# Order of the loads on GpSimd's queue in an attention and mixture kernel: q and k ahead of v, weight halves behind

## The chip, the cores and the metric

The kernel runs on one core of a Trainium2 chip. The metric is the device time of one execution in microseconds. The engines are called as in the profile: PE (matrix products), DVE (vector), ACT (activations and copies), POOL (GpSimd) and SP. All loads are issued by POOL, and their descriptors go to one queue; SP issues the stores of the result.

## The reference

An attention with an extra term in the denominator, for 8 batches of 12 heads with 448 tokens of 64 values, and behind it a soft mixture of 8 experts with 4 slots each. Cut to what matters:

```
scores = q @ k.T / sqrt(64);  m = max(scores);  e = exp(scores - m)
attn = e / (sum(e) + exp(-m) + 1e-9);  x = attn @ v          # x: 3584 x 768
logits = x @ phi                                             # 3584 x 32
d = softmax over the tokens;  slot_in = d.T @ x               # 32 x 768
slot_out[e] = relu(slot_in[e] @ w1[e]) @ w2[e]                # w1: 768x1024, w2: 1024x768
out = softmax over the slots(logits) @ slot_out
```

## The kernel before, in words

The work is cut into 48 pairs of heads, and three pairs make a group g (16 groups, two for each batch). One slot s of the main loop (L556) does the work of one pair, in two halves y; the order of the instructions on every engine is the order in which the code writes them, since the schedule is made by hand. The main parts are these:

- T(n) (L193) transposes q and k of pair n on PE: 14 transposes of q, then 14 of k, for 7 parts of the tokens and the two heads. In slot s from 2 on, y = 1 calls T(s + 6), so the transposes run six pairs ahead of the pair's exponentials.
- A(n, i) (L216) computes scores on PE (L225, L235) and takes their maxima on DVE (L229, L238). W1(g) (L241) writes the negated maxima of a group on POOL (L245), W2 and W3 turn them (PE L265, L266, ACT L271).
- Bk(n, i) (L281) computes the transposed scores less the maxima on PE (L300, L303) and the exponentials on ACT (L306); AV (L319) multiplies them with v on PE (L331).
- N1 and N2 (L337, L346) divide by the sums: a copy on ACT (L343), two small operations on DVE (L352, L353), three on POOL (L359, L367, L368). PX (L382) turns the result. P(b) (L404) does the logits of a batch in steps that are spread over later slots; its subtractions are on POOL (c_sub L437, d_sub L449), and the exponential of what they write is on ACT (L454).
- V(g) (L310) copies v of a group on POOL (L312 to L315) into a padded layout. It is called in each slot with s % 3 == 0.

The loads stand between these on POOL's stream. load(g, "q") and load(g, "k") (L141) fetch a whole group, cast to 16 bits, into one of two buffers, chosen by g % 2; T(n) reads it. load(g, "v") (L145, L146) fetches v into one buffer, from which V copies. The 16 weight matrices come as halves: the first eleven into a tile W of their own, a first half with load_half(i, 0) in the slots s = 1, 4, 7, 10, 13, 16, 22, 25, 28, 31, 34 and the second half one slot later (L108); the other five go into the space of R when attention has left it (from s = 38 on).

At the end of each slot, POOL gets its loads in this order (L607 to L626): in slots with s % 3 == 0, V, then v for the group after, then q and k of group s / 3 + 3; in slots with s % 3 == 1 (after W1) a first weight half; in slots with s % 3 == 2 a second half. q and k of group 3 are loaded in slot 1. POOL works through its stream in order, so an issue that waits holds up everything behind it.

After the main loop come the last products of P (L468), the experts (hidden L646, turn L657, slots L663), and the combination with the result's stores (L715 to L737).

Of the kernel before, what the change touches and what calls it, by code (L numbers as in the profile page):

```python
# [31 lines left out]
def kernel(  # L32
# [22 lines left out]
    NG = NPAIR // NP  # L55
# [45 lines left out]
    def w_view(i, t):  # L101
        kind, e = halves[i]
        w_sb[(kind, e)] = t.rearrange("p (j f) -> p j f", f=F if kind == "w1" else DD)

    def load_part(i, z0, z1):
        kind, e = halves[i]
        src = (moe_w1 if kind == "w1" else moe_w2)[e].rearrange("(j p) f -> p j f", p=128)
        gdma(out=w_sb[(kind, e)][:, z0:z1, :], in_=src[:, z0:z1, :])  # L108

    def load_half(i, z, t=None):  # L110

        if t is not None:
            w_view(i, t)
        n = (KC if halves[i][0] == "w1" else FK) // 2
        load_part(i, z * n, (z + 1) * n)
# [6 lines left out]
    with ExitStack() as at:  # L122
# [10 lines left out]
        def load(g, nm, l0=0, l1=NP):  # L133


            b, h0 = g // 2, (g % 2) * HG
            src = {"q": q, "k": k, "v": v}[nm][b, h0:h0 + HG]
            if nm != "v":
                t = part(f"nq{g % 2}", "qk".index(nm) * NP * S, NP * S).rearrange("p (l x) -> p l x", l=NP)
                x = src.rearrange("(l h) (j t) d -> (h j) l (t d)", h=2, t=7)  # L140
                gdma(out=t[:, l0:l1, :], in_=x[:, l0:l1, :])  # L141
            else:
                t = part("nv", 0, NATV).rearrange("p (h t d) -> p h t d", h=HG, t=4)
                x = src.rearrange("h (p t) d -> p h t d", t=7)
                gdma(out=t[0:64], in_=x[:, :, 0:4, :])  # L145
                gdma(out=t[64:128], in_=x[:, :, 3:7, :])  # L146
            nat[nm, g] = t
# [45 lines left out]
        def T(n):  # L193
            g, pl = divmod(n, NP)
            ps = psA.tile([128, 2, S], BF16, tag="a", name="ps_t")
            for a in range(2):
                src = nat["qk"[a], g]
                for tok in range(7):
                    for hl in range(2):

                        c = kcol(hl, tok) if a else (2 * tok if tok < 4 else 2 * tok - 7) * 64
                        r = slice(64 * hl, 64 * hl + 64)
                        nc.tensor.transpose(ps[r, a, c:c + 64], src[r, pl, tok * D:(tok + 1) * D], ident[r, r])  # L203
            t = qk_t[n % NQK]
            if n < 6 or pl == 0:
                nc.scalar.copy(t, ps)  # L206
            else:
                nc.vector.tensor_copy(t, ps)
            qkT[n] = t
# [31 lines left out]
        def W1(g):  # L241
            w, m = wm[g % 2], mx[g]
            l0, l1 = mpl(g)
            nm = psm.tile([128, 21], BF16, tag="ngm", name="ngm")
            neg = lambda o, s: nc.gpsimd.tensor_scalar(o, s, -1.0, None, op0=ALU.mult)  # L245
            cols = lambda t: t[:, 0:3 * HG].rearrange("p (i c) -> p i c", i=3)[:, :, 2 * l0:2 * l1]
            o = w[:, 0:3, :].rearrange("p i (d c) -> p i d c", d=2)[:, :, :, 2 * l0:2 * l1]
            neg(o, cols(m).unsqueeze(2).to_broadcast([128, 3, 2, 2 * (l1 - l0)]))
            for hl in range(2):
                r = slice(64 - 64 * hl, 128 - 64 * hl)  # L250
                o = w[r, 3, :].rearrange("p (d c) -> p d c", d=2)[:, :, 2 * l0 + hl:2 * l1:2]
                neg(o, m[r, 3 * HG + l0:3 * HG + l1].unsqueeze(1).to_broadcast([64, 2, l1 - l0]))
            if l1 - l0 == NP:
                neg(nm, m)
            else:
                nc.gpsimd.memset(nm, 0.0)
                neg(cols(nm), cols(m))
                neg(nm[:, 3 * HG + l0:3 * HG + l1], m[:, 3 * HG + l0:3 * HG + l1])
            ngm[g] = nm
# [21 lines left out]
        def Bk(n, i, c=0):  # L281

            g, pl = divmod(n, NP)
            t = qkT[n]
            rs = [slice(0, 64), slice(64, 128)]
            if i < 3:
                pss = [pb_("ps_b") for _ in range(2)]
                outs = [p[:, 0:S] for p in pss]
                cols = slice(i * 128, (i + 1) * 128)
                e = e2_t[st["e2"] % NE]  # L290
                st["e2"] += 1
                es = [e[:, hl, :] for hl in range(2)]
            else:
                pss = [pb_("ps_b")]
                outs = [pss[0][r, 0:S] for r in rs]
                cols = slice(384, 448)
                es = [e1_t]
            m = cols.stop - cols.start
            for hl in range(2):
                nc.tensor.matmul(outs[hl], t[rs[hl], 1, cols], t[rs[hl], 0, :], start=True, stop=False)  # L300
            As(c)
            for hl in range(2):
                nc.tensor.matmul(outs[hl], sel[rs[hl], 2 * pl + hl:2 * pl + hl + 1].to_broadcast([64, m]), mT[mg(n)][rs[hl], :],  # L303
                                 start=False, stop=True)
            for p, e in zip(pss, es):
                nc.scalar.activation(e, p[:, 0:S], AF.Exp, scale=scale)  # L306
            for hl in range(2):
                eT[n, i, hl] = es[hl % len(es)]
# [221 lines left out]
        def As(c):  # L530
            for _ in range(min(c, len(runs))):
                A(*runs.pop(0))
# [19 lines left out]
        half_at = {s: i for i, s in enumerate((1, 4, 7, 10, 13, 16, 22, 25, 28, 31, 34))}  # L552
# [3 lines left out]
        for s in range(NPAIR + 1):  # L556
            for y in range(2):
                hs = 2 * s + y
                early = int(hs < 5)
                As(1)  # L560
                if s < NPAIR:
                    Bk(s, 2 * y)
                    As(early)
                    side = int(y == 1 and len(runs) > 0 and runs[0][1] == 3)
                    Bk(s, 2 * y + 1, side)
                    As(1 - side)
                else:
                    As(1)
                if hs == 1:
                    W1(1)  # L570
                if hs < 5:
                    T(hs + 3)
                if y == 0:
                    if 0 <= s - 1:
                        for i in (2, 3):
                            AV(s - 1, i, range(3))
                else:
                    if 2 <= s < NPAIR - 6:
                        T(s + 6)
                    g = (s + 1) // 3  # L580
                    if (s + 1) % 3 == 0 and g < NG:
                        W2(g + 1)
                        W3(g + 1)
                    if s < NPAIR:
                        for i in (0, 1):
                            AV(s, i, range(3))
                if 2 * s + y in post:
                    post[2 * s + y]()
                if y and 0 <= s - 2 < NPAIR - 2:
                    PX(s - 2)  # L590
                if y == 0:
                    if 0 <= s - 1:
                        for i in range(4):
                            AV(s - 1, i, [3])
                        N1(s - 1)
                        if not on_pool(s - 1):
                            N2(s - 1)
                else:
                    if 0 <= s - 1 and on_pool(s - 1):
                        N2(s - 1)  # L600
                As(early)
                if hs == 1:
                    W2(1)
                    W3(1)
                if hs == 4:
                    W1(2)
            g = (s + 9) // 3  # L607
            if s % 3 == 0 and g - 2 < NG:
                V(g - 2)
                if s and g - 1 < NG:  # L610
                    load(g - 1, "v")
            if s == 1 or (s and s % 3 == 0):
                if g < NG:
                    load(g, "q")
                    load(g, "k")
            if s % 3 == 1:
                if 1 < (s + 2) // 3 < NG:
                    W1((s + 2) // 3 + 1)
                if s == 1:
                    load(2, "v")  # L620
            if s in half_at:
                load_half(half_at[s], 0, w_tile(half_at[s]))
            if s - 1 in half_at:
                load_half(half_at[s - 1], 1)
            for i, z0, z1 in part_at.get(s, ()):
                load_part(i, z0, z1)  # L626
        load_part(14, 1, 8)
# [140 lines left out]
```

## Time and profile before

| | |
|---|---|
| median of 3 runs | 326.14 us (326.11 to 327.19) |
| the profiled execution | 328.46 us |
| its span, first to last instruction | 326.7 us |
| busy share: PE, DVE, ACT, POOL | 86%, 79%, 77%, 61% |
| mean granted clock of PE | 0.96 |
| share of 16 DMA engines taken by the loads' queue | 85.1% |
| loads of q or k of a whole group: each, median from issue to landing | 336 KB, 7.1 us (q), 8.1 us (k) |
| half of a weight matrix | 768 KB, 9.2 us |

How to read it: busy times are those of one profiled execution. A timeline row has start and length in us, engine, line and operation, and in brackets how long the engine stood idle before it and what ended that. A row of the chain has start, length and what was working. A row of waits has who waited for what, us in total, how many times, and the longest. The size of a load is what it writes (16 bits a value); it reads twice that. A windows row has the stretch, its length, the busy time of PE, PE's weight loads, DVE, ACT and POOL with counts of instructions, the granted clock, the share of the DMA engines and GB/s.

### The profile page before, as it was taken

How to read it: one execution, taken by the hardware profiler on the slowest of the kernel's cores; microseconds unless marked ns; L12 is line 12 of the kernel's file. 1: busy time of each engine (PE TensorE's matmuls, PEld its weight loads, DVE VectorE, ACT ScalarE, POOL GpSimd, SP SyncE). 2: the span in 40 equal slices, each digit the busy share in tenths (PEclk: the TensorE clock that was granted, in tenths of full speed). 3: DMA queues.
4: the chain of work that ended last, by engine and by line, in shares of the span. 5: the costliest groups of instructions: out<-in, count | busy, mean ns of one | idle time of the engine just before them, and what ended most of it. 6: DMA issues, size and time to landing. Idle time of an engine off the chain costs nothing.

```text
span 326.7 us, 12121 instructions
## 1 busy us (share of the span) xinstructions
PE 281.9 (86%) x5054; PEld 162.9 (50%) x5054; DVE 257.8 (79%) x601; ACT 251.1 (77%) x547; POOL 198.1 (61%) x399
## 2 busy tenths in 40 slices
PE   3898899899999999899989999999999987987800
PEld 1444456556556565556555655556564544452100
DVE  5779999798999899889988998999999365337910
ACT  2457699989999899889988999899989986317800
POOL 8640769777778868585978597859666734100000
PEclk9999999999999999999999999999999999999555
DMA  7990699999999999759999999999934899983997
GB/s 93 131 132 3 91 208 149 203 171 170 158 181 169 183 176 158 102 64 175 137 181 169 171 153 177 170 184 142 144 50 70 136 153 176 210 159 148 442 421 337
DMA packets 42438, 54.30 MB, mean 166 GB/s; under 512 B 2576, under 2 KB 35344, under 8 KB 42000
## 3 DMA queue, kind: packets, MB, share of 16 engines
q0 software_dynamic: 41376, 42.52, 85.1%
q1 hardware_dynamic: 1008, 11.01, 8.0%
q8 instruction: 39, 0.64, 0.7%
q14 instruction: 15, 0.12, 0.1%
HBM read 85.03 MB, written 11.01 MB: 294 GB/s over the span
## 4 chain that ended last, share of the span: by engine, by line
PE 32%; DVE 24%; ACT 11%; POOL 11%; DMA 11%; issue 6%; POOLq 0%; ACTq 0%; DVEq 0%
DVE mx L229 14%; DMA R<-in_k_dram 11%; PE ps_av L331 6%; ACT R L306 5%; PE ps_a L225 5%; PE ps_b L300 4%; PE ps_t L203 4%; PE ps_b L303 3%; DVE mx L238 2%; ACT W L732 2%; PE ps_o L726 2%; ACT R L206 2%; PE ps_h L653 2%; PE ps_so L667 2%; PE ps_s L469 2%
## 5 line engine op out<-in xcount | busy, mean ns | idle before, releaser
L229 DVE TENSOR_REDUCE mx<-ps_a 128x1 f32<-128x448 f32 x288 | 160.4, 613 | 15.7 <-PE ps_a L225 15.2
L306 ACT ACTIVATE R<-ps_b 128x448 bf16<-128x448 f32 x336 | 158.2, 559 | 13.2 <-PE ps_b L303 8.9
L300 PE MATMUL ps_b<-R 64*128 64x448 bf16 (+1 forms) x384 | 83.0, 360 | 2.2 <-ACT R L397 2.0
L303 PE MATMUL ps_b<-mT,sel 64*128 64x448 bf16 (+1 forms) x384 | 79.0, 354 | 0.0
L225 PE MATMUL ps_a<-R 64*128 64x448 bf16 x288 | 68.8, 369 | 5.8 <-DVE mx L229 3.9
L359 POOL TENSOR_TENSOR R<-ubuf,rec 128x384 bf16<-128x384 f32 x44 | 36.2, 823 | 53.3 <-DVE rec L353 45.2
L331 PE MATMUL ps_av<-R 128*128 128x65 bf16 (+1 forms) x1536 | 64.8, 196 | 1.4 <-DVE ubuf L343 1.3
L331 PEld LDWEIGHTS <-R 128*128 128x128 bf16 (+1 forms) x1536 | 50.6, 101 | 27.5 <-issue 23.5
L203 PEld LDWEIGHTS <-R 64*64 64x64 bf16 x1344 | 31.8, 113 | 23.2 <-issue 9.6
L203 PE MATMUL ps_t<-ident,R 64*64 64x64 bf16 x1344 | 32.9, 198 | 10.8 <-DMA R<-in_q_dram 4.3
L397 ACT CAST R<-ps_x 128x512 bf16<-128x512 f32 x47 | 28.1, 598 | 10.1 <-PE ps_x L391 10.1
L300 PEld LDWEIGHTS <-R 64*128 64x128 bf16 (+1 forms) x384 | 19.7, 97 | 27.5 <-issue 23.0
L303 PEld LDWEIGHTS <-sel 64*128 64x128 bf16 (+1 forms) x384 | 21.5, 98 | 23.4 <-issue 16.8
L238 DVE TENSOR_REDUCE mx<-ps_a 128x1 f32<-128x448 f32 x48 | 29.4, 614 | 0.6 <-PE ps_a L235 0.3
L206 ACT COPY R<-ps_t 128x896 bf16<-128x896 bf16 x20 | 18.3, 915 | 12.9 <-PE ps_t L203 12.9
L343 ACT COPY ubuf<-ps_av 128x455 f32<-128x455 f32 x44 | 25.0, 569 | 2.1 <-PE ps_av L331 1.0
L225 PEld LDWEIGHTS <-R 64*128 64x128 bf16 x288 | 17.8, 94 | 15.1 <-issue 4.1
L368 POOL TENSOR_TENSOR R<-ubuf,rec 128x128 bf16<-128x128 f32 x44 | 17.5, 398 | 3.7
L235 PE MATMUL ps_a<-R 64*64 64x448 bf16 x96 | 18.7, 385 | 0.6 <-DVE mx L229 0.6
L245 POOL TENSOR_SCALAR R<-mx 64x6 bf16<-64x6 f32 (+5 forms) x51 | 13.5, 264 | 8.6 <-DVE mx L229 5.0
L391 PE MATMUL ps_x<-ident,R 128*128 128x128 bf16 x192 | 18.7, 219 | 0.0
L108 POOL DMA_DIRECT2D W<-in_moe_w_dram x22 | 17.9, 814 | 0.7 <-issue 0.7
(121 smaller groups left out, 357.3 us busy)
## 6 DMA issues: line engine op xcount, KB each, us to landing
W<-in_moe_w_dram POOLq DMA_DIRECT2D x22, 768.0 KB, 9.2
out_dram<-W SPq DMA_DIRECT2D x3, 2688.0 KB, 11.4
R<-in_v_dram POOLq DMA_DIRECT2D x32, 192.0 KB, 4.8
R<-in_q_dram POOLq DMA_DIRECT2D x15, 336.0 KB, 7.1
R<-in_k_dram POOLq DMA_DIRECT2D x15, 336.0 KB, 8.1
R<-in_moe_w_dram POOLq DMA_DIRECT2D x3, 768.0 KB, 8.7
out_dram<-W SPq DMA_DIRECT2D x3, 768.0 KB, 4.3
R<-in_moe_w_dram POOLq DMA_DIRECT2D x1, 1344.0 KB, 11.9
```

The source lines that it names most:

```text
L203: nc.tensor.transpose(ps[r, a, c:c + 64], src[r, pl, tok * D:(tok + 1) * D], ident[r, r])
L206: nc.scalar.copy(t, ps)
L225: nc.tensor.matmul(pss[hl][:, 0:S], t[r, 0, i * 128:(i + 1) * 128], t[r, 1, :], start=True, stop=True)
L229: nc.vector.reduce_max(mx[g][:, c:c + 1], pss[hl][:, 0:S], axis=AX.X)
L238: nc.vector.reduce_max(mx[g][:, c:c + 1], ps[:, 0:S], axis=AX.X)
L300: nc.tensor.matmul(outs[hl], t[rs[hl], 1, cols], t[rs[hl], 0, :], start=True, stop=False)
L303: nc.tensor.matmul(outs[hl], sel[rs[hl], 2 * pl + hl:2 * pl + hl + 1].to_broadcast([64, m]), mT[mg(n)][rs[hl], :], start=False, stop=True)
L306: nc.scalar.activation(e, p[:, 0:S], AF.Exp, scale=scale)
L331: nc.tensor.matmul(o, eT[n, i, hl][:, qc], vp[g % 2][:, 2 * pl + hl, i, 0:W65], start=(i == 0 and u == 0 and hl == 0), stop=(i == 3), skip ...
L343: (nc.scalar.copy if on_pool(n) else nc.vector.tensor_copy)(u, src)
L359: eng.tensor_mul(x[:, 0:3, c:c + 128].rearrange("p i (h d) -> p i h d", h=2), u[:, 0:6, 0:D].rearrange("p (i h) d -> p i h d", h=2), rec[: ...
L397: nc.scalar.copy(xT[:, pb, :], pss[0])
```

## The change

The block at the end of a slot is put in another order. In slots with s % 3 == 2 (from s = 2 on) q and k of group (s + 10) // 3 are loaded; before, the same group's were loaded one slot later, behind V and the load of v. Group 3 is loaded in slot 1 as before. The second half of a weight matrix is loaded two slots behind the first, in place of one, so in slots with s % 3 == 0, behind v. So on POOL's stream the two loads of q and k and the second weight half change places. Since V's wait for PE no longer stands ahead of them, the issues of q and k carry a wait of their own for PE's T(s + 6), the last reader of the buffer that they fill.

```diff
+            g = (s + 10) // 3
+            if s == 1 or s % 3 == 2:
+                g = 3 if s == 1 else g
+                if (s == 1 or g > 3) and g < NG:
+                    load(g, "q")
+                    load(g, "k")
             g = (s + 9) // 3
             if s % 3 == 0 and g - 2 < NG:
                 V(g - 2)
                 if s and g - 1 < NG:
                     load(g - 1, "v")
-            if s == 1 or (s and s % 3 == 0):
-                if g < NG:
-                    load(g, "q")
-                    load(g, "k")
...
             if s in half_at:
                 load_half(half_at[s], 0, w_tile(half_at[s]))
-            if s - 1 in half_at:
-                load_half(half_at[s - 1], 1)
+            if s - 2 in half_at:
+                load_half(half_at[s - 2], 1)
```

## The prediction

> **What bounds the kernel now.** I read the chain that ended last (the page's fourth part, then in order of time), PE's waits, the transposes in PE's timeline, and POOL's timeline around one group of loads.
>
> ```profile
> PE 32%; DVE 24%; ACT 11%; POOL 11%; DMA 11%; issue 6%; POOLq 0%; ACTq 0%; DVEq 0%
> DVE mx L229 14%; DMA R<-in_k_dram 11%; PE ps_av L331 6%; ACT R L306 5%; PE ps_a L225 5%; PE ps_b L300 4%; PE ps_t L203 4%; PE ps_b L303 3%; DVE mx L238 2%; ACT W L732 2%; PE ps_o L726 2%; ACT R L206 2%; PE ps_h L653 2%; PE ps_so L667 2%; PE ps_s L469 2%
> ```
>
> No engine holds the chain alone, but one transfer has 11% of it, the load of k. In order of time it stands there four times; these are the first and the last (start, length, what).
>
> ```profile
> 82.00 8.86 DMA R<-in_k_dram
> ...
> 193.00 8.86 DMA R<-in_k_dram
> ```
>
> That share, some 36 us, is the way of the chain and not the price: it runs beside PE, DVE and ACT at work. The price is what PE waits. PE's waits (in total, times, longest):
>
> ```profile
> PE ps_t L203 <- DMA R<-in_k_dram: 2.8, 4, 1.1
> ...
> PE ps_m L266 <- POOL z L437: 0.4, 1, 0.4
> ```
>
> PE stood four times for k, 2.8 us together. Whether another engine makes that good is seen in the transposes of one pair after the other, each row a T(n), one in each slot (start, length; in brackets the idle time before):
>
> ```profile
> 43.95 0.63 PE L203 MATMUL ps_t<-ident,R 64*64 64x64 bf16 x28
> 48.91 0.63 PE L203 MATMUL ps_t<-ident,R 64*64 64x64 bf16 x28
> ...
> 58.48 0.41 PE L203 MATMUL ps_t<-ident,R 64*64 64x64 bf16 x14
> ...
> 64.30 0.63 PE L203 MATMUL ps_t<-ident,R 64*64 64x64 bf16 x28
> ...
> 105.84 0.60 PE L203 MATMUL ps_t<-ident,R 64*64 64x64 bf16 x28
> ...
> 111.31 0.63 PE L203 MATMUL ps_t<-ident,R 64*64 64x64 bf16 x28 [0.51 <-DVE mx L229]
> ...
> 116.53 0.63 PE L203 MATMUL ps_t<-ident,R 64*64 64x64 bf16 x28
> ...
> 137.05 0.38 PE L203 MATMUL ps_t<-ident,R 64*64 64x64 bf16 x14
> 138.16 0.41 PE L203 MATMUL ps_t<-ident,R 64*64 64x64 bf16 x14 [0.73 <-DMA R<-in_k_dram]
> ...
> 143.25 0.63 PE L203 MATMUL ps_t<-ident,R 64*64 64x64 bf16 x28 [0.58 <-DVE mx L229]
> ...
> 169.12 0.38 PE L203 MATMUL ps_t<-ident,R 64*64 64x64 bf16 x14
> ...
> 175.34 0.63 PE L203 MATMUL ps_t<-ident,R 64*64 64x64 bf16 x28 [0.58 <-DVE mx L229]
> ...
> 201.26 0.38 PE L203 MATMUL ps_t<-ident,R 64*64 64x64 bf16 x14
> ...
> 207.05 0.63 PE L203 MATMUL ps_t<-ident,R 64*64 64x64 bf16 x28 [0.64 <-DVE mx L229]
> ```
>
> At 137.05 q's half of T(27) runs at once and k's half stands until 138.16. From T(27) to T(28) go 143.25 - 137.05 = 6.20 us. The same slot two groups sooner, T(21) to T(22), did not wait for a load: 111.31 - 105.84 = 5.47. The difference of 0.73 is the whole wait, so nothing made it good. In the same way T(33) gives 175.34 - 169.12 - 5.47 = 0.75, and T(39) 207.05 - 201.26 - 5.47 = 0.32. For T(12), in the early slots, T(9) is the measure: (64.30 - 58.48) - (48.91 - 43.95) = 5.82 - 4.96 = 0.86. By spacing the four cost 2.66 us; by the row of waits 2.8.
>
> **The change part by part.** Only POOL's instructions change places; the other engines keep their order. Here is POOL before, slots 17 to 20:
>
> ```profile
> 120.78 0.80 POOL L108 DMA_DIRECT2D W<-in_moe_w_dram  x1
> 123.23 0.82 POOL L359 TENSOR_TENSOR R<-ubuf,rec 128x384 bf16<-128x384 f32 x1 [1.65 <-DVE rec L353]
> ...
> 126.78 0.72 POOL L145 DMA_DIRECT2D R<-in_v_dram  x1
> ...
> 128.15 0.78 POOL L141 DMA_DIRECT2D R<-in_q_dram  x1
> 128.90 0.79 POOL L141 DMA_DIRECT2D R<-in_k_dram  x1
> 129.75 0.82 POOL L359 TENSOR_TENSOR R<-ubuf,rec 128x384 bf16<-128x384 f32 x1
> ...
> 135.13 0.40 POOL L368 TENSOR_TENSOR R<-ubuf,rec 128x128 bf16<-128x128 f32 x1
> 136.44 0.52 POOL L449 TENSOR_TENSOR z<-lb,lb 128x160 f32<-128x160 f32 x1 [0.91 <-DVE lb L445]
> ```
>
> *q and k sooner.* Groups 4 to 15, twelve of them, are issued where the second weight half stood: q at 120.78 in place of 128.15, k at 120.78 + 0.78 = 121.56 in place of 128.90, 7.3 us sooner. Landings around this place, one issue each, in the order W half of 116.68, q, k, and last the slowest load of the kernel's end (KB, us to landing):
>
> ```profile
> W<-in_moe_w_dram POOLq DMA_DIRECT2D x1, 768.0 KB, 9.0
> ```
> ```profile
> R<-in_q_dram POOLq DMA_DIRECT2D x1, 336.0 KB, 7.2
> R<-in_k_dram POOLq DMA_DIRECT2D x1, 336.0 KB, 9.2
> ```
> ```profile
> R<-in_moe_w_dram POOLq DMA_DIRECT2D x1, 576.0 KB, 12.5
> ```
>
> Before, q landed at 128.15 + 7.2 = 135.35 and k at 138.1, so each takes the queue some 2.75 us. After, the half issued at 116.68 is ahead and lands at 125.7; then q and k, by 125.7 + 2 x 2.75 = 131.2 (estimate). With the 12.5 of the slowest load it would be 134.1. T(27) wants k after 137.05. Both ends are in time, with 3 to 6 us over, so all four waits go. Value: 2.7, bounds 2.66 and 2.8.
>
> The Trainium skill ("DMA: Bandwidth & Descriptors", Anatomy of one DMA) gives one load from GpSimd 2.0 us and the bytes at 436 GB/s, which makes an estimated 2.8 us for 336 KB. By that rule k of 128.90 would land at 131.7, before PE wants it, and moving it would bring nothing here. The row shows 9.2, and PE's wait names this load, so the trace disagrees: the load stands in a queue.
>
> *The wait that comes with it.* The new issue waits until PE has transposed the group that last used the buffer, in the same slot: T(23), over at 116.53 + 0.63 = 117.16. POOL comes there at 120.78, 3.6 us later, so it doesn't stand. If that cover went, N2 of the next pair and V would queue behind it. Cost nothing.
>
> *POOL in the slot of the new issue.* Two issues (0.78 + 0.79) for one (0.80): 0.77 us more. N2 at 123.23 follows after 1.65 us idle, which hides it; without the cover V and v would be 0.77 late, and v is read a group later. In every second group L449 stands behind the issue; in slot 20 the two issues go from 135.53 to 137.1, so it starts some 0.6 us later than 136.44. Its reader:
>
> ```profile
> 141.68 0.44 ACT L454 ACTIVATE cd<-z 128x256 bf16<-128x256 f32 x1
> ```
>
> It has over 4 us. Cost nothing; without that cover 0.6 in each of six groups.
>
> *POOL in the next slot.* One issue (0.80) for two: N2 at 129.75 starts about 0.75 sooner, and W1 behind it. This can remove the wait of PE at L266, 0.4 us by its row, since the chain comes to it over POOL, through the issue
>
> ```profile
> 64.89 1.31 POOL R L141 x2
> ```
>
> Value 0.1, since DVE work may end last there; bounds 0 and 0.4.
>
> *Second weight halves later.* Each of eleven is issued some 7.4 us later, after v. The last, issued at about 224, lands by 224 + 12.5 = 236.5. The first product that reads weights for the result:
>
> ```profile
> 281.27 4.07 PE ps_h L653 x72
> ```
>
> Over 40 us of cover; cost nothing. Late next, after k: the step DVE L229 to T(n) (0.51 to 0.64 idle in the rows above), which is in the undisturbed slots too and stays.
>
> Sum: 2.7 + 0.1 = 2.8 us; the span goes from 326.7 to 323.9. The profiled execution took 328.46, 1.8 more than its span; the median of the timed runs is 326.14, 2.3 below it. I take the gain off the median: **323.3 us**.
>
> **Rivals.**
>
> *Absorbed.* Once k is there, another engine is late and half the gain stays: 326.14 - 1.4 = 324.7. For it speaks that all three are nearly full in such a stretch (125 to 141; busy PE, PEld, DVE, ACT, POOL):
>
> ```profile
> 125.00:141.00 16.00, 15.13 (x304) 9.44 (x303) 14.32 (x34) 14.59 (x34) 11.91 (x25) 1.00 0.76 112
> ```
>
> Against it: the undisturbed slots run at 5.47 with the same work. Chance 0.16.
>
> *More goes than the waits*, by 3.6 or more: 322.3 with L266 and POOL's earlier N2 in several groups. Chance 0.04.
>
> *Nothing moves.* q and k are issued sooner but land as late, or the four waits were not k's and stay: 326.1. The 0.73 idle for k, as long as the slot was longer, speaks against it. Chance 0.04. The rule of the Trainium skill on one load (above) belongs here.
>
> *Slower: the queue.* A second half, issued behind v, is now followed by a first half and 4 us later by q and k, so q and k have up to two halves ahead where before they had v and what was left of one. It decides when k takes over 15.5 us (121.56 to 137.05). At 17 us each of twelve groups would stand 1.5 us: 326.14 - 2.8 + 18 = 341. The slowest landing is 12.5, in another stage. Chance 0.04.
>
> *Slower: the clock.* It falls to half at 300.8, after PE's last dense stage (length, then busy PE first; the clock is the third number from the end):
>
> ```profile
> 282.00:296.70 14.70, 12.88 (x245) 6.91 (x237) 4.42 (x13) 4.49 (x8) 0.00 (x0) 1.00 0.79 143
> ...
> 300.80:312.00 11.20, 8.29 (x37) 1.37 (x33) 10.16 (x11) 8.32 (x10) 0.00 (x0) 0.50 1.05 435
> ```
>
> Were it to fall at 282, PE's 12.9 us there would double: 336; it outweighs the gain where it falls with over 2.8 us of that work to come. The Trainium skill ("TensorE: Matmul & The Clock Gate", What's actually happening) has a free-running window of 3413 ns, so a start shifted by 2.8 us may meet it otherwise. By that rule the moment could differ; the three times of before lie within 1.1 us, and their trace shows one fall. Chance 0.04.
>
> **How the numbers follow.** Forecast 0.68 (gain 2.2 to 3.6), absorbed 0.16, the other four 0.04 each. The range takes the forecast and nearly all of absorbed: 322.4 to 325.6; it takes in 323.0 (gain 3.1, both upper bounds). A measurement of this kernel tells 0.5%, 1.6 us, from no change, so faster means below 324.5: 0.68 + 0.04 + half of absorbed = 0.80; same 0.08 + 0.04 = 0.12; slower 0.08.
>
> **What would show it.** Right: no PE wait for k after group 3, k issued right behind N2 in slots 2, 5, 8 and on; k gone from the chain; slots T(12), T(27), T(33), T(39) as long as their undisturbed ones; k's landing under 12 us. Wrong: PE idle before T(n) for a load or for DVE in new places, L454 late behind L449, POOL idle before the issue of q, or the clock falling ahead of the last products.

## The result and the profile after

The changed kernel takes 324.12 us (median of 17 runs, 323.03 to 326.12). The kernel before, run beside it, takes 326.26 us (17 runs, 325.31 to 329.66). The ratio is 0.9935, 95% interval 0.9914 to 0.9957: faster, by 2.1 us. The forecast was 323.3 with a gain of 2.8. One execution of the kernel called q and k alone below took 573.5 us and is left out of its ratio. The profiled execution after took 326.12 with a span of 324.3; before it was 328.46 and 326.7.

The page of after, its chain that ended last (by engine, then by line):

```profile
PE 35%; DVE 29%; ACT 18%; issue 6%; DMA 4%; POOL 3%; POOLq 0%; ACTq 0%
DVE mx L229 18%; ACT R L306 9%; PE ps_av L331 8%; PE ps_a L225 6%; PE ps_b L300 6%; PE ps_t L203 5%; DMA R<-in_moe_w_dram 4%; PE ps_b L303 4%; ACT R L206 3%; DVE mx L238 3%; ACT R L397 2%; PE ps_o L728 2%; DVE R L208 2%; ACT W L734 2%; PE ps_s L469 2%
```

The load of k, 11% of the chain before, is gone from it. A single transfer is left, a part of the last weights, with 4%. PE's waits after (total, times, longest):

```profile
PE ps_so L669 <- DMA R<-in_moe_w_dram: 0.8, 1, 0.8
...
PE ps_av L331 <- issue: 0.6, 1, 0.6
...
PE ps_m L266 <- POOL R L245: 0.3, 1, 0.3
```

No row names k. Two rows are new: 0.8 for the last weights, and 0.6 for which the trace names no releaser ("issue"). POOL after, in the slot of the new issues (slot 17):

```profile
119.11 0.81 POOL L141 DMA_DIRECT2D R<-in_q_dram  x1
119.93 0.77 POOL L141 DMA_DIRECT2D R<-in_k_dram  x1
...
121.44 0.82 POOL L359 TENSOR_TENSOR R<-ubuf,rec 128x384 bf16<-128x384 f32 x1 [0.74 <-DVE rec L353]
...
126.37 0.78 POOL L108 DMA_DIRECT2D W<-in_moe_w_dram  x1
```

The issue of q has no bracket: POOL did not stand for the new wait. N2 behind the issues still starts after idle time (0.74, before 1.65), so the extra issue is hidden. These two loads land so (KB, us from issue to landing):

```profile
R<-in_q_dram POOLq DMA_DIRECT2D x1, 336.0 KB, 6.7
R<-in_k_dram POOLq DMA_DIRECT2D x1, 336.0 KB, 7.5
```

k is there at 119.93 + 7.5 = 127.4, nearly 8 us before T(27) wants it. Last, PE's transposes at the four places of the prediction, and T(11) ahead of them:

```profile
53.43 0.63 PE L203 MATMUL ps_t<-ident,R 64*64 64x64 bf16 x28
...
58.15 0.63 PE L203 MATMUL ps_t<-ident,R 64*64 64x64 bf16 x28
...
63.12 0.63 PE L203 MATMUL ps_t<-ident,R 64*64 64x64 bf16 x28
...
135.26 0.60 PE L203 MATMUL ps_t<-ident,R 64*64 64x64 bf16 x28
...
136.76 0.31 PE L331 MATMUL ps_av<-R 128*128 128x65 bf16 x5 [0.58 <-issue]
...
141.28 0.63 PE L203 MATMUL ps_t<-ident,R 64*64 64x64 bf16 x28 [0.70 <-DVE mx L229]
...
167.03 0.60 PE L203 MATMUL ps_t<-ident,R 64*64 64x64 bf16 x28
...
172.50 0.63 PE L203 MATMUL ps_t<-ident,R 64*64 64x64 bf16 x28 [0.51 <-DVE mx L229]
...
198.25 0.60 PE L203 MATMUL ps_t<-ident,R 64*64 64x64 bf16 x28
...
203.73 0.63 PE L203 MATMUL ps_t<-ident,R 64*64 64x64 bf16 x28 [0.51 <-DVE mx L229]
```

T(12) to T(13) is 4.97 (measure: 4.96), T(33) to T(34) 5.47 and T(39) to T(40) 5.48 (measure: 5.47). Three waits are gone to a hundredth. T(27) to T(28) is 6.02: k is there, but a wait for "issue" of 0.58 stands in its place. T(11) to T(12) is 4.72, and before, where T(11) stands at

```profile
53.44 0.63 PE L203 MATMUL ps_t<-ident,R 64*64 64x64 bf16 x28
```

it was 58.48 - 53.44 = 5.04; no load was waited for there. That is a gain in one slot, where the prediction had 0.1 for all slots.

**The table on which the rest stands.** In the eight profiles of the two kernels PE's clock opened at 18.3 to 24.3 us and was not halved before 271.7, so from T(11) to T(47) it is full. The work of a slot is the same in every execution, and the distance from one T(n) to the next repeats to some hundredths unless something was late. From here on, slot n is the stretch from T(n) to T(n+1); T(n) is called in the loop's slot n - 6, so this count runs six ahead of the loop's own. The slots that tell the kernels apart or that stood for k, in us (the last three columns are kernels of the next section):

| n | before, first profile | before, four more profiles | after, three profiles | q and k alone | halves alone | POOL filled |
|---|---|---|---|---|---|---|
| 11 | 5.04 | 5.04 to 5.06 | 4.72, 4.73, 4.73 | 4.72 | 5.81 | 5.13 |
| 12 | 5.82 | 4.96 to 5.18 | 4.97, 4.96, 4.96 | 4.97 | 4.96 | 4.96 |
| 14 | 5.83 | 5.31 to 5.41 | 5.32, 5.32, 5.32 | 5.35 | 5.90 | 5.41 |
| 15 | 4.80 | 4.80 to 5.01 | 4.80, 4.80, 4.80 | 4.80 | 4.80 | 4.80 |
| 18 | 4.91 | 4.91 to 5.27 | 4.91, 4.91, 4.94 | 4.91 | 4.91 | 4.91 |
| 20 | 5.42 | 5.32 to 5.59 | 5.31, 5.35, 6.01 | 5.32 | 5.96 | 5.32 |
| 26 | 5.32 | 5.31 to 5.32 | 5.32, 5.32, 5.32 | 5.31 | 5.95 | 5.31 |
| 27 | 6.20 | 5.47 to 6.06 | 6.02, 5.47, 5.79 | 5.48 | 6.37 | 5.47 |
| 32 | 5.45 | 5.45 to 5.47 | 5.31, 5.32, 5.31 | 5.32 | 5.97 | 5.32 |
| 33 | 6.22 | 5.47 to 5.59 | 5.47, 5.47, 5.48 | 5.48 | 5.48 | 5.47 |
| 36 | 4.91 | 4.91 to 5.03 | 4.91, 4.91, 4.91 | 4.91 | 5.35 | 4.91 |
| 38 | 5.48 | 5.38 to 5.52 | 5.31, 5.31, 5.32 | 5.32 | 5.54 | 5.72 |
| 39 | 5.79 | 5.47 to 5.80 | 5.48, 5.48, 5.47 | 5.49 | 5.48 | 5.47 |
| 44 | 5.46 | 5.31 to 5.32 | 5.31, 5.32, 5.32 | 5.36 | 5.98 | 5.31 |
| 45 | 5.46 | 5.47 to 6.05 | 5.47, 5.47, 5.48 | 5.48 | 6.49 | 5.48 |
| T(11) to T(47) | 190.20 | 187.46 to 188.49 | 186.73, 186.44, 187.48 | 186.35 | 193.29 | 187.13 |

### The profile page after: what moved, and what is told of

Its sections match the earlier page's. It is cut to its first block, busy times and chain, and to the rows that moved or that the text cites. A ratio compares the mean times of both kernels' runs of the same rounds, so it can differ in the third digit from the quotient of the medians.

```text
span 324.3 us, 12137 instructions
## 1 busy us (share of the span) xinstructions
PE 281.0 (87%) x5052; PEld 162.5 (50%) x5054; DVE 257.5 (79%) x601; ACT 250.3 (77%) x547; POOL 199.3 (61%) x399
## 4 chain that ended last, share of the span: by engine, by line
PE 35%; DVE 29%; ACT 18%; issue 6%; DMA 4%; POOL 3%; POOLq 0%; ACTq 0%
DVE mx L229 18%; ACT R L306 9%; PE ps_av L331 8%; PE ps_a L225 6%; PE ps_b L300 6%; PE ps_t L203 5%; DMA R<-in_moe_w_dram 4%; PE ps_b L303 4%; ACT R L206 3%; DVE mx L238 3%; ACT R L397 2%; PE ps_o L728 2%; DVE R L208 2%; ACT W L734 2%; PE ps_s L469 2%
## 5 line engine op out<-in xcount | busy, mean ns | idle before, releaser
L203 PE MATMUL ps_t<-ident,R 64*64 64x64 bf16 x1344 | 31.9, 198 | 7.7 <-DMA R<-in_q_dram 4.0
L245 POOL TENSOR_SCALAR R<-mx 64x6 bf16<-64x6 f32 (+5 forms) x51 | 13.5, 264 | 8.4 <-DVE mx L229 4.8
L108 POOL DMA_DIRECT2D R<-in_moe_w_dram x15 | 10.7, 717 | 12.3 <-PE ps_s L469 7.2
```

## The experiments

My theory after the result: k's waits went, and POOL's earlier N2 and W1 gave more than I had put down. Rivals: the second halves' place does the work; the waits for k are as large in every execution and part of the gain is absorbed; the new wait for the last weights, or the clock, takes back what is missing.

**after again, and after a third time.** No edit; the first was timed and profiled, the second only profiled.

> The changed kernel once more, unaltered, as the measure for the other three. Theory: T(47) starts near 240.2 us again, 3.5 sooner than before, and PE again stands some 0.8 us for the last weight load behind slots (the tail gives part of the gain back); a time near 324.1. The 0.58 us that PE stood after T(27) without a cause in the profile comes from no change of order, so it should be gone or at another place. Rival: the wait at the end was an accident of that one execution; then it is absent here and the span is 323.2.

> A third profile of the changed kernel. Theory: no wait for k and T(11) to T(47) at 186.3 to 186.7, whatever the clock does at the start; the wait for the last weight load, seen in one of its two profiles, is rare and so absent here.

The first gave 324.19 us, ratio 0.992 (0.9891 to 0.9949), span 323.2; the second 324.49 in its one execution, span 322.7. Neither has a wait for k or for the last weights. T(27) of the first repeat:

```profile
134.86 0.60 PE L203 MATMUL ps_t<-ident,R 64*64 64x64 bf16 x28
...
140.33 0.63 PE L203 MATMUL ps_t<-ident,R 64*64 64x64 bf16 x28 [0.51 <-DVE mx L229]
```

It is 5.47, so the 0.58 was that one execution's own. The second repeat has the like in slot 20 (1.0) and again in 27 (0.3), by PE's waits:

```profile
PE ps_av L331 <- issue: 1.2, 2, 1.0
```

**before, four times more.** No edit. Each one profile, to see whether 2.8 us of waits for k is what the kernel has or what one execution had.

> The kernel before once more, for a second profile of it. Theory, that the times differ from run to run with the moment at which PE's clock opens at the start (24.3 in the first profile of before, 18.4 to 24.1 in the others) and with a dip of one 3.4 us window near 272 to 278: the slots from T(11) on repeat the first profile within 0.3 us, with waits for k of 2 to 3 us in all, and the slots T(3) to T(5) are shorter by as much as the clock opens sooner. Rival, that the waits for k in the first profile were unusually long: then they are under 1.5 us here, and the gain of the change in the usual run is smaller by that.

> A third profile of the kernel before, with the same expectations as the second: k waited for by 2 to 3 us (theory) or under 1.5 us (rival); start and dip of the clock as they fall.

> A fourth profile of the kernel before. Theory, that its waits for k differ from one execution to the next and set how long the main loop takes: T(11) to T(47) between 187.5 and 190.2, longer by about as much as the waits for k are longer (2.8 us gave 190.2, 1.7 gave 188.5, 0.8 gave 187.7). Rival, that they are tied to the moment at which the clock opens at the start: late opening with long waits, early opening with short ones.

> A fifth profile of the kernel before, with the expectations of the fourth.

PE's waits for k in these four, in order:

```profile
PE ps_t L203 <- DMA R<-in_k_dram: 1.7, 4, 0.6
```
```profile
PE ps_t L203 <- DMA R<-in_k_dram: 0.8, 2, 0.5
```
```profile
PE ps_t L203 <- DMA R<-in_k_dram: 0.2, 1, 0.2
```
```profile
PE ps_t L203 <- DMA R<-in_k_dram: 0.4, 1, 0.4
```

They took 325.5, 324.54, 325.13 and 326.39 us. Together with the first profile's 2.8 the mean is 5.9 / 5 = 1.2 us. The waits are real and fall on changing slots, and the profile on which the prediction stands had the longest of five. The main loop grows with them: in the order of the waits, 0.2, 0.4, 0.8, 1.7 and 2.8 us, T(11) to T(47) took 187.46, 187.53, 187.74, 188.49 and 190.20; as far as five executions show, nothing made them good.

**q and k alone.** The loads of q and k move; the second halves stay one slot behind the first.

```diff
-            if s - 2 in half_at:
-                load_half(half_at[s - 2], 1)
+            if s - 1 in half_at:
+                load_half(half_at[s - 1], 1)
```

> Only q and k one slot sooner; the second weight half stays one slot behind the first and so stands right behind q and k. Theory (k must land before PE wants it; POOL's shorter work behind V helps too): no wait for k, N2 behind v starts another 0.8 us sooner, T(47) at 240.2 or up to 0.3 sooner, and the end again held by the last weight load: 323.6 to 324.3. Rival (the gain comes from moving the second halves out of the way of q and k): no different here, since the half is behind q and k, so this run does not tell it apart, halves_only does. A second rival (a slot with three issues holds up V): V and N2 0.8 late in slots 3, 6 and on, and T(47) 0.5 or more later than with both parts.

324.84 us, ratio 0.9935 (0.9906 to 0.9965). No wait for k; its slots are those of after (table). The 0.65 us to the whole change on the same chip lies inside the intervals.

**Halves alone.** The kernel before, with the second halves two slots behind.

```diff
-            if s - 1 in half_at:
-                load_half(half_at[s - 1], 1)
+            if s - 2 in half_at:
+                load_half(half_at[s - 2], 1)
```

> Only the second weight halves one slot later, behind q and k; q and k stay behind V and v. Theory, that k must land sooner by whatever means: k of group 9 is issued at 128.9 as before but has only v ahead, lands near 134.5 in place of 138.1, before the 137.05 at which PE comes to it, so the four waits go (2.7 us); but POOL then has five issues behind V, and N2 of the next slot comes 0.8 later, which costs up to 1.0 in the slots where POOL is on the chain: 324.5 to 325.8. Rival, that only the sooner issue counts: the waits stay and the time is 326 to 327.

329.57 us, ratio 1.0095 (1.0068 to 1.0122): slower, where I had expected a gain. So the two parts are not two gains: the move of q and k alone gives the gain, as far as the intervals tell, and the halves' move by itself costs 3 us. PE's waits name k and POOL:

```profile
PE ps_t L203 <- DMA R<-in_k_dram: 2.3, 3, 1.0
...
PE ps_m L266 <- POOL R L245: 2.3, 7, 0.3
...
PE ps_m L265 <- POOL R L245: 0.6, 1, 0.6
```

First k. POOL's rows at group 9's k:

```profile
128.28 0.78 POOL L141 DMA_DIRECT2D R<-in_k_dram  x1
129.04 0.77 POOL L108 DMA_DIRECT2D W<-in_moe_w_dram  x1
```

and the landing of the two loads issued there:

```profile
R<-in_q_dram POOLq DMA_DIRECT2D x1, 336.0 KB, 7.9
R<-in_k_dram POOLq DMA_DIRECT2D x1, 336.0 KB, 10.0
```

The half that was issued at 116.67 landed 11.6 us later, at 128.3, just as k was issued; from there on only v and q were ahead of k. It still took 10.0 us, more than the 9.2 that the prediction shows for it, where I had expected it to land sooner. The half that is issued 0.76 us behind k is not shown to be the cause: a half stands in the same place behind group 8's k, which landed after 7.3 us,

```profile
R<-in_k_dram POOLq DMA_DIRECT2D x1, 336.0 KB, 7.3
```

and in q and k alone a half is issued 0.77 us behind k, too, which landed after 6.7 to 8.7. In this kernel k took 7.3 to 10.2 us over the eleven groups with a half right behind it, and 7.8 in the one without. Why three of them took 9.5 and more stays open. The waits for k, 2.3 us, lie within the 0.2 to 2.8 of before: moving the halves out of the way of k does not take them away, and only its sooner issue did.

Then POOL's own time. Behind V stand five issues in a row in place of four, and W1's masks (L245) come late. PE's product with the last of them, L266, in slot 11, first POOL and then PE of this kernel:

```profile
52.86 0.97 POOL L245 TENSOR_SCALAR R<-mx 128x36 bf16<-128x36 f32 x3
```
```profile
53.23 0.34 PE L265 MATMUL ps_m<-ident,R 128*128 128x128 bf16 x3 [0.56 <-POOL R L245]
53.89 0.20 PE L266 MATMUL ps_m<-ident,R 128*128 128x64 bf16 x1 [0.32 <-POOL R L245]
```

The masks are done at 52.86 + 0.97 = 53.83 and L266 starts at 53.89. In the slots 14, 20, 26, 32 and 44 L266 stands in the same way; each is 0.58 to 0.66 longer than in the repeat of after, twice what the row of waits says (0.32 each), since the products just ahead of it stand for the masks before, in gaps too short for the row. From T(11) to T(47) this kernel is 193.29 - 186.44 = 6.85 us longer than the repeat: 2.4 in the slots 27, 36 and 45, which wait for k, and 4.4 in the slots 11, 14, 20, 26, 32, 38 and 44, most of them with L266 late after POOL. Against the medians of before those seven slots are 3.7 longer, so the loss is mainly POOL's. The profiled execution took 331.05, 1.5 above the median of its kernel.

**POOL filled.** After, with three memsets of a scratch tile behind the load of v, so that POOL's slot is as full as it was, while q and k stay where the change put them.

```diff
                     load(g - 1, "v")
+                    for _ in range(3):
+                        nc.gpsimd.memset(fill, 0.0)
```

> The changed kernel with three memsets on POOL behind v in slots 3, 6, to 39, some 0.7 us together, about what the change had taken out of that slot. Theory, that 1.3 us of the gain in the main loop came from POOL's earlier N2 and W1: T(47) starts some 1.0 to 1.4 later than in the changed kernel, while k is still never waited for; the end, held by the last weight load, takes up most of it, so the time is only 0.3 to 0.8 longer. Rival, that POOL's time there is hidden and the whole gain was k's: T(47) within 0.2 of the changed kernel and the same time.

324.89 us, ratio 0.9943 (0.9911 to 0.9974). In time it can't be told from the whole change (324.19 on that chip), but the slots tell it. Slot 11 in the three kernels, POOL and PE of before, of after, and of this one:

```profile
53.50 0.97 POOL L245 TENSOR_SCALAR R<-mx 128x36 bf16<-128x36 f32 x3
```
```profile
54.52 0.20 PE L266 MATMUL ps_m<-ident,R 128*128 128x64 bf16 x1 [0.18 <-POOL R L245]
```
```profile
52.74 0.97 POOL L245 TENSOR_SCALAR R<-mx 128x36 bf16<-128x36 f32 x3
```
```profile
54.16 0.19 PE L266 MATMUL ps_m<-ident,R 128*128 128x64 bf16 x1
```
```profile
53.37 0.97 POOL L245 TENSOR_SCALAR R<-mx 128x36 bf16<-128x36 f32 x3
```
```profile
54.40 0.20 PE L266 MATMUL ps_m<-ident,R 128*128 128x64 bf16 x1 [0.27 <-POOL R L245]
```

T(11) starts at 53.44, 53.43 and 53.23, so L266 comes 1.08, 0.73 and 1.17 after it. Filling POOL brings back the 0.32 of this slot and a little more (5.13), and 0.41 in slot 38, again at L266. Slot 14 is 0.10 longer, too. That is 0.9 by the slots, less than the 1.0 to 1.4 that I had expected. It doesn't bring back the 0.14 of slot 32. So POOL's earlier masks are shown as a cause for slot 11; slot 32 has another (last section).

**No last load.** After without the load of the last part of the last weights.

```diff
-        load_part(15, 5, 8)
```

> The changed kernel without the last weight load (the last 3 of 8 row blocks of the second matrix of the eighth expert, 576 KB; the products read what stood there before). Theory A, that the end gives back what the main loop gained because the last weight load lands late: 0.8 to 1.1 us less than the changed kernel, about 323.2. Theory B, that the late landing in the first profile of the changed kernel was one execution's own: within 0.4 us of the changed kernel.

324.14 us, ratio 0.9937 (0.9908 to 0.9965): the same as with it. In the first profile of after PE stood there, in the timeline:

```profile
291.47 1.14 PE L669 MATMUL ps_so<-R,W 128*32 128x384 bf16 x21 [0.76 <-DMA R<-in_moe_w_dram]
```

The load was issued 13.9 us ahead of its landing there and 11.7 in the repeat, where nobody waited. It is no new bound.

**A warmer clock, late and early.** Two kernels for the 0.8 us that the forecast is below the result. In the first, PE is kept busy for eight products in place of two, whose result nobody reads, behind the last pair; in the second also eighteen such products in the first slots.

```diff
-        keep_busy(2)
+        keep_busy(8)
```

> The changed kernel with six more idle products on PE where it waits 1.55 us for ACT in the last batch, which keep the clock's window from falling. Theory (a dip of one window there costs some 0.85 us in about half of the executions, whatever the loads do): no dip in the trace, a spread of times without the upper group, median 0.3 to 0.6 us under the changed kernel, near 323.8. Rival: the dip costs nothing at the end, or the products push the step behind them; same or 0.3 longer.

```diff
+        fill(6)
...
+        fill(8)
...
-        As(2)
+        As(1)
+        fill(4)
+        As(1)
```

> The kernel of the run warm with 18 more idle products of 128 columns on PE in the first 10 us, in stretches where PE waits for q, for ACT or for DVE, so that the clock opens sooner. Theory (the clock opens at the end of a busy window, at 18.0 to 24.3 so far, and each us that it opens later costs about 0.25 us between T(3) and T(11)): the clock opens before 18, T(3) to T(11) takes 34.5 or less, and the median falls to about 323.2. Rival: the few products do not fill a window, or delay T(0) and T(1): opening at 18 to 24 as before and 324.2 to 324.6.

324.38, ratio 0.993 (0.9901 to 0.996), and 324.15, ratio 0.993 (0.9905 to 0.9955). Neither beats the plain change. In the second the clock opened at 18.8 us, where I had expected less than 18, so it didn't do what it was built for. What the first aims at can be seen in the repeat of after, in three stretches near its end (length, busy PE first; the clock is the third number from the end):

```profile
267.90:271.30 3.40, 1.90 (x41) 1.26 (x39) 2.40 (x11) 1.56 (x5) 2.01 (x4) 1.00 1.16 212
271.70:275.10 3.40, 3.36 (x20) 1.58 (x16) 0.72 (x2) 0.64 (x2) 1.51 (x4) 0.51 1.15 207
275.20:277.70 2.50, 2.22 (x34) 1.18 (x33) 1.47 (x6) 0.43 (x2) 0.18 (x1) 1.00 1.14 205
```

For 3.4 us the clock is halved. The stage from T(47) to the end then takes 84.0 us in place of 83.1. One of the five profiles of before has it and one of the three of after, so it can't be called part of the change. With more products there the granted clock of every run was 0.957 or higher (six of the twelve runs of the repeat had 0.952 or 0.953), but the median did not fall.

## Why the prediction was right, and where its sizes were off

- **The waits for k go: right, term mis-sized.** All are gone, in each of the profiles with q and k moved, and in the profiled pair three of the four slots came out to a hundredth as worked out (0.85, 0.75, 0.31 against 0.86, 0.75, 0.32); the fourth did in the repeat (0.73). But "Value: 2.7, bounds 2.66 and 2.8" was the price of one execution. Over five it was 0.2 to 2.8, mean 1.2. The warning stood in the table: that execution took 2.3 us more than the median of the runs. The waits were part of that; another part was the clock, which opened at 24.3 us, later than in the other four (from T(3) to T(11) 36.11 us, against 34.64 to 35.91). Then "I take the gain off the median" took waits off a time that does not hold them all.
- **POOL's next slot: the direction right, "Value 0.1 ... bounds 0 and 0.4" too small.** W1's masks came 0.75 us sooner, as worked out (L245 in slot 11 at 53.50, then 52.74). The worth over the main loop is some 0.8: 0.32 in slot 11, 0.14 in 32, 0.17 in 38, and by the medians of the five some 0.1 each in 14 and 20. I had read one wait's row of 0.4 and then taken a quarter of it. The row was the wrong measure: slot 14's extra 0.4 was that one execution's, and slot 11's row shows 0.18 where the slot gained 0.32.
- **The sum.** 1.2 + 0.8 = 2.0 against the measured 2.1 (1.4 to 2.8 by the interval). The one term was too large by 1.5 and the other too small by 0.7, and the two errors work against each other: that the time came out inside the range is in part luck. The gain of 2.1 lies just under the 2.2 to 3.6 that the forecast stood for. The profiles give less in the main loop, 188.3 - 186.9 = 1.4 by the means of five and of three; the waits for "issue" in those of after are 0.6 longer in the mean, as much as is missing. Two figures of the working are off without moving the range: both upper bounds make 3.2 and not 3.1, and 3.6 off the median is 322.5 and not 322.3.
- **The new wait, the slot of the new issue, the second halves: right at nothing.** POOL is not idle ahead of the issue of q. L449 starts 5.50 us after T(20) in place of 5.03, some 0.5 later (0.6 was worked out), and ACT's waits name z after POOL's work in neither kernel. Nobody waits for a second half. That the halves' move costs nothing holds only together with the move of q and k: alone it costs 0.95%.
- **The queue: the conclusion right, the model wrong.** k lands at 127.4, sooner than the estimate of 131.2. The 2.75 us for each load came from one pair of rows: in the same profile q's landing and k's are 1.6 to 1.7 us apart in nine of the twelve groups, and 2.6 to 2.8 in three, group 9 among them. By it I expected halves alone to lose its waits for k, and it kept them. What makes a load slow in some groups isn't shown.
- **Absorbed.** The result, 324.12, is nearer to this rival's 324.7 than to the forecast's 323.3, but not by its way: the slots that stood for k are as short as undisturbed ones, so what was taken away was gained whole. *Nothing moves* and *the queue* fell. *The clock* did not fall earlier in a way that belongs to one kernel.

**Open.** The waits for "issue" (0.3, 0.6 and 1.4 us in the three profiles of after; none, none, 0.3, none and 0.5 in those of before) have no cause in the trace. In the other kernels with q and k moved they are none (q and k alone, POOL filled), 0.2 (no last load), 0.4 and 1.2 (warmer clock, late and early), so whether the change brings more of them can't be said from so few. Whether the halves' move adds anything to that of q and k isn't settled (0.65 us, within the intervals).

## What to carry to other kernels

Profile the kernel before more than once ahead of pricing a wait for a load: a wait that changes its slot has a mean, and one profile gives a sample of it; where that execution's time is above the median, the waits may be part of why, and so may the clock. In a loop that repeats, measure the distance of the same instruction from slot to slot, not the rows of waits: it repeats to hundredths, shows what was not made good, and shows gains where no row stands. Moving two issues past each other on one engine gives and takes at both places, so try each half of such a change by itself.

## What the runs showed of the hardware that I had not expected

A small DVE instruction is held up beside POOL. L352 reads two tiles of 128x7; all its instances, of before and then of after (ns, shortest, median, longest):

```profile
L352 DVE SCALAR_TENSOR_TENSOR rec<-ubuf,ec x47: 134/154/370, 32.6 to 271.2; 128x7 f32<-128x7 f32 x47
```
```profile
L352 DVE SCALAR_TENSOR_TENSOR rec<-ubuf,ec x47: 132/155/167, 32.5 to 267.7; 128x7 f32<-128x7 f32 x47
```

The longest of before, in slot 38, and what POOL did then (in all five profiles of before L352 takes 0.27 to 0.40 us in the slots 32 and 38, each time beside L437):

```profile
197.46 0.37 DVE L352 SCALAR_TENSOR_TENSOR rec<-ubuf,ec 128x7 f32<-128x7 f32 x1
```
```profile
197.38 0.41 POOL L437 TENSOR_TENSOR z<-lb,cm 128x128 f32<-128x128 f32 x1
```

It ends with POOL's instruction, 197.83 and 197.79. In slot 38 PE's product L442, two steps on, is then 0.12 late and the slot 0.17 longer. After, POOL is there sooner, no instance is longer than 0.17 in its three profiles, and the 0.14 of slot 32 and the 0.17 of slot 38 are gone. In q and k alone it moved to other places: two instances take 0.52 and 0.54, beside L449 in the slots 33 and 39. The Trainium skill ("SBUF — State Buffer", Who interferes with whom) says that a DVE instruction with two inputs in SBUF contends with a GpSimd instruction that reads SBUF, and the one that comes second is blocked. The rows agree here. In slot 20 of before, though, the like falls beside an issue of a load:

```profile
102.10 0.30 DVE L352 SCALAR_TENSOR_TENSOR rec<-ubuf,ec 128x7 f32<-128x7 f32 x1
```
```profile
101.88 0.83 POOL L108 DMA_DIRECT2D W<-in_moe_w_dram  x1 [0.69 <-issue]
```

An issue alone doesn't do it, for in slot 11 of before L352 lies wholly within one and takes its usual time:

```profile
54.90 0.15 DVE L352 SCALAR_TENSOR_TENSOR rec<-ubuf,ec 128x7 f32<-128x7 f32 x1
```
```profile
54.65 0.83 POOL L108 DMA_DIRECT2D W<-in_moe_w_dram  x1
```

What held it in slot 20 is open. That L352 is held by POOL's L437 is read from such pairs of rows; no run tried it by itself.
